# Turned attention weights: one transfer to DRAM and four back, in place of 16 transfers within SBUF

## The chip, the cores and the metric

The kernel runs on one core of one Trainium2 chip. The metric is the device time of one execution in microseconds (us); the figure is the median of three runs. The engines are called by the names that the profile uses: PE (TensorE, matrix products), DVE (VectorE), ACT (ScalarE), POOL (GpSimd) and SP (SyncE, which here does nothing but issue transfers). SPq is SP's queue of instructions, PEld the loading of weights into PE.

## The reference: what is computed

An attention that keeps only the 32 largest scores of each row, then a feed-forward block. All data are float32.

```python
B, H, S, D = 8, 8, 576, 64                    # batches, heads, sequence, head dim
scores = scale * q @ k.T                      # per batch and head: 576 x 576
kth    = np.partition(scores, -32)[..., -32]  # the 32nd largest of each row
scores = np.where(scores >= kth, scores, -1e9)
attn   = softmax(scores)                      # weights z: 576 queries x 576 keys
x      = (attn @ v)                           # then heads side by side: 4608 x 512
h      = x @ w_in                             # 4608 x 2048
out    = (h - np.tanh(h)) @ w_out             # 4608 x 512
```

## The kernel before

The kernel goes through the problem in 144 steps. A step takes 128 queries of two heads (of one batch), or the 64 queries that remain of two pairs of heads. A step runs through a pipeline over several iterations of one loop: scores on PE, the search for the 32nd largest score on DVE, mask and exponential on ACT and POOL, and then the product with v on PE. For that product the keys have to lie on the partitions, while the weights come out with the queries on the partitions. So the weights are turned.

For batch 0 PE turns them (`turn_pe`, steps with `pe`). For all others DVE turns each block of 32 x 32 within its group of 32 partitions, and transfers then bring the blocks to the groups where they belong. Two steps (a pair, `nq == 2`) share one such exchange; the remainders (`rem`, `nq == 1`) have one each.

```python
zx2 = [consts.tile([P, 4 * S], FP32, name="zx")[:], later[:, 0 : 4 * S]]   # two buffers
et_rem = later[:, 4 * S : 6 * S]          # "later" is part of the tile "spare"
etpool = pool("et", 1)                    # one buffer
G, NG = 32, 4                             # partitions in a group, groups
...
def turn_z(n):                            # DVE: turn 32 x 32 blocks
    g, z = steps[n], st.pop(n)["z"]
    ...
    nc.vector.transpose(
        tiles(zx, g.nq)[:, :, :, g.i, :].rearrange("p c k j -> p k c j"),
        z[:].rearrange("p (k c j) -> p k c j", c=NG, j=G),
    )

def spread_keys(n):                       # 16 transfers: group a, column block c
    zx = zxs.pop(n)                       #   -> group c, column block a
    rem = steps[n].rem
    et = ets[n] = et_rem if rem else etpool.tile([P, 4 * S], FP32, tag="et", name="et")
    w = steps[n].nq * S // 2              # 576 for a pair, 288 for a remainder
    for a in range(NG):
        for c in range(NG):
            nc.sync.dma_start(
                et[group(c), a * w : (a + 1) * w], zx[group(a), c * w : (c + 1) * w]
            )

def values(n):                            # PE: product with v, from et
    ...
    nc.tensor.matmul(av[half(t), 0, cols], vb[g.b, hp][:, t, c, :] ..., es[...], ...)
```

The order of instructions is fixed by hand. In iteration `n` of the loop stand, among others and in this order:

```python
    for m in (n - 4, n - 3):              # lag is 4 for steps turned by transfers
        if 0 <= m < NS and steps[m].last and steps[m].lag == n - m:
            values(m)                     # PE: weights of step n - 4
    ...
    if here(0):
        search(n, exact, between)         # DVE; after its first round: turn_z(n - 2)
    if here(-2) and not pe and steps[n - 2].last:
        spread_keys(n - 2)                # SP
    deal(...)                             # PE: a share of the feed-forward products
    if here(1):
        scores(n + 1)                     # PE
    ...
    for fn in todo.pop(n, []):
        fn()                              # SP: loads of k, q, v for later steps
```

So the weights of a pair are turned and sent out in iteration n and used at the start of iteration n + 2. `search` reads the scores straight from PSUM (one buffer there), so the scores of the next step wait for its first operations. All transfers of this stretch are issued by SP, in the order of the program: the exchange, the loads and the results.

Of the kernel before, what the change touches and what calls it, by code (L numbers as in the profile page):

```python
# [10 lines left out]
FP32 = mybir.dt.float32  # L11
# [37 lines left out]
def kernel(  # L49
# [9 lines left out]
    nc = tc.nc  # L59
    P = nc.NUM_PARTITIONS  # L60
# [10 lines left out]
    NG = P // G  # L71
    KC = 2 * S // P
    G = 32
    NG = P // G
# [8 lines left out]
    def pool(name, bufs, **kw):  # L83
        return ctx.enter_context(tc.tile_pool(name=name, bufs=bufs, **kw))
# [10 lines left out]
    xrpool = pool("xr", 1)  # L95
    thpool = pool("th", 4)
    gpool = pool("g", 4)
    sc_ps = pool("sc_ps", 1, space=PS)
    zt_ps = pool("zt_ps", 2, space=PS)
    h_ps = pool("h_ps", 2, space=PS)  # L100
# [260 lines left out]
    def group(a):  # L361
        return slice(a * G, (a + 1) * G)
# [18 lines left out]
    def spread_keys(n):  # L381


        zx = zxs.pop(n)
        rem = steps[n].rem
        et = ets[n] = et_rem if rem else etpool.tile([P, 4 * S], FP32, tag="et", name="et")
        w = steps[n].nq * S // 2
        for a in range(NG):
            for c in range(NG):
                nc.sync.dma_start(  # L390
                    et[group(c), a * w : (a + 1) * w], zx[group(a), c * w : (c + 1) * w]
                )

    def turn_pe(n):

# [137 lines left out]
    steps, done, work = [], {}, []  # L533
# [36 lines left out]
    def run(exact):  # L570
# [119 lines left out]
        for n in range(-4, NS + 4):  # L690
# [16 lines left out]
            if here(-2) and not pe and steps[n - 2].last:  # L707
                spread_keys(n - 2)
# [64 lines left out]
```

## Time and profile before

| What | before |
|---|---|
| time, median of 3 runs | 1543.8 us (1543.63 to 1544.71) |
| span of the profiled run | 1542.8 us |
| PE busy | 1440.7 us (93%) |
| DVE busy | 1347.2 us (87%) |
| ACT busy | 883.9 us (57%) |
| POOL busy | 940.8 us (61%) |
| bytes moved by DMA | 147.42 MB, mean 96 GB/s |
| exchange of a pair, `et<-zx` and `et<-spare` | 896 transfers of 72 KB |
| exchange of a remainder, `spare<-zx` and `spare<-spare` | 224 transfers of 36 KB |

How to read it: an engine's busy time is a sum over the whole span, and the span has stages. The weights of the feed-forward block are loaded and converted at the start, batch 0 is turned on PE, from about 255 us on the exchange is done by transfers, and in the last 100 us only PE has much left to do. A name such as `et<-zx` is a transfer or an operation that writes `et` and reads `zx`; `L390` is the line of the exchange in the kernel, `L376` the turn on DVE, `L433` the product with v, `L486` and `L507` the two products of the feed-forward block, `L237` the scores. The two buffers of `zx` appear under two names, `zx` and `spare`.

### The profile page before, as it was taken

To read this page: it belongs to the slowest core of one execution; us is meant where nothing else is said; L and a number is where in the kernel's file an instruction comes from. 1 tells how busy PE (TensorE), PEld (TensorE's weight loads), DVE (VectorE), ACT (ScalarE), POOL (GpSimd) and SP (SyncE) were. 2 spreads that over 40 slices of the span, in tenths; PEclk is the share of its full clock that TensorE was granted. 3 is DMA by queue.
4 is the path that set the end of the run, shared out by engine and by line. 5 is a ranking of instruction groups with operands and counts; after the bars stand their busy time and mean duration, and the time that the engine had idled before them with its cause. 6 is when DMAs were issued, how large, how long until landed. Compare 5 with 4: busy or idle time off the path is not lost.

```text
span 1542.8 us, 25300 instructions
## 1 busy us (share of the span) xinstructions
PE 1440.7 (93%) x7428; PEld 912.1 (59%) x7428; DVE 1347.2 (87%) x3828; ACT 883.9 (57%) x1567; POOL 940.8 (61%) x1525
## 2 busy tenths in 40 slices
PE   2567899999999999999999999999999999999997
PEld 1355566465666666656566665656566665656673
DVE  6998899999999999999999999999999999997300
ACT  4887776566555565556555565556555565655320
POOL 2777677567665665756565675757565675746420
PEclk9887999999999999999999999999999999999999
DMA  9944113324533354234433354234433344322200
GB/s 241 360 169 168 50 32 76 78 71 102 112 86 80 76 112 101 70 79 95 106 87 79 77 110 103 70 78 96 102 89 79 77 103 109 78 67 58 73 8 16
DMA packets 258835, 147.42 MB, mean 96 GB/s; under 512 B 210048, under 2 KB 217216, under 8 KB 258688
## 3 DMA queue, kind: packets, MB, share of 16 engines
q1 hardware_dynamic: 256912, 145.49, 38.5%
q8 instruction: 62, 1.02, 0.3%
q14 instruction: 85, 0.70, 0.1%
q10 hardware_dynamic: 1776, 0.22, 0.1%
HBM read 61.85 MB, written 9.44 MB: 46 GB/s over the span
## 4 chain that ended last, share of the span: by engine, by line
PE 73%; DVE 10%; SPq 5%; ACT 4%; DMA 2%; issue 2%; POOL 2%; DVEq 0%; ACTq 0%; POOLq 0%
PE ops L507 28%; PE hps L486 26%; PE av L433 9%; PE scps L237 8%; SPq L390 3%; DVE m L275 2%; DVE ab L278 2%; PE av L441 2%; SPq L200 2%; DMA zx<-in_moe_w_in_dram 1%; DVE spare L376 1%; PE zt L409 1%; DVE ab L267 1%; DVE ab L270 1%; DVE ab L268 1%
## 5 line engine op out<-in xcount | busy, mean ns | idle before, releaser
L507 PE MATMUL ops<-w_out,g 128*128 128x512 f32 x1152 | 520.5, 598 | 0.0
L486 PE MATMUL hps<-xT,w_in 128*128 128x256 f32 (+1 forms) x2176 | 471.4, 372 | 1.2 <-POOL xT L457 1.2
L275 DVE MAX8 m<-ab 128x8 f32<-128x288 f32 (+1 forms) x1152 | 465.8, 447 | 0.0
L310 POOL TENSOR_TENSOR z<-sc,z 128x576 f32<-128x576 f32 x288 | 400.2, 1411 | 77.4 <-ACT z L307 77.4
L486 PEld LDWEIGHTS hps<-xT,w_in 128*128 128x128 f32 x2176 | 390.7, 193 | 73.9 <-issue 23.4
L278 DVE MATCH_REPLACE8 ab<-m,ab 128x288 f32<-128x288 f32 x864 | 377.3, 446 | 0.0
L507 PEld LDWEIGHTS ops<-w_out,g 128*128 128x128 f32 x1152 | 211.4, 191 | 244.8 <-issue 240.7
L307 ACT ACTIVATE z<-sc,tb 128x576 f32<-128x576 f32 x288 | 207.6, 769 | 153.1 <-POOL tb L294 153.1
L500 POOL TENSOR_TENSOR g<-g,th 128x512 f32<-128x512 f32 x144 | 183.7, 1276 | 123.5 <-ACT g L499 113.2
L330 ACT ACTIVATE z<-z,nb 128x576 f32<-128x576 f32 x288 | 221.6, 773 | 8.8 <-POOL z L310 8.7
L245 ACT COPY sc<-scps 128x1152 f32<-128x1152 f32 x144 | 160.9, 1117 | 108.5 <-PE scps L237 106.5
L237 PE MATMUL scps<-kT,qT 64*128 64x288 f32 (+1 forms) x1280 | 188.1, 445 | 31.7 <-DVE qT L222 28.1
L237 PEld LDWEIGHTS scps<-kT,qT 64*128 64x128 f32 (+1 forms) x1280 | 101.6, 184 | 120.5 <-issue 60.5
L267 DVE TENSOR_TENSOR ab<-scps,sc 128x576 f32<-128x576 f32 x144 | 108.0, 750 | 69.3 <-POOL bad L314 54.1
L433 PE MATMUL av<-et,vb 128*64 128x256 f32 (+1 forms) x1088 | 131.8, 378 | 37.2 <-ACT et L412 30.4
L457 POOL TENSOR_TENSOR xT<-xs 128x256 f32<-128x256 f32 (+1 forms) x68 | 47.2, 695 | 166.8 <-ACT xs L445 166.8
L498 ACT ACTIVATE th<-hps 128x512 f32<-128x512 f32 x144 | 85.4, 593 | 106.6 <-PE hps L486 104.1
L445 ACT COPY xs<-av 128x512 f32<-128x512 f32 (+1 forms) x84 | 44.2, 526 | 170.2 <-PE av L441 170.2
L433 PEld LDWEIGHTS av<-et,vb 128*64 128x64 f32 x1088 | 75.2, 139 | 98.6 <-ACT et L412 32.5
L340 POOL TENSOR_SCALAR rd<-den 128x2 f32<-128x2 f32 x144 | 33.4, 232 | 140.5 <-ACT z L330 98.2
L270 DVE MAX8 ab<-ab 128x8 f32<-128x288 f32 x288 | 116.9, 448 | 0.0
L268 DVE TENSOR_TENSOR ab<-scps,sc 128x576 f32<-128x576 f32 x144 | 107.8, 749 | 0.0
(67 smaller groups left out, 1253.9 us busy)
## 6 DMA issues: line engine op xcount, KB each, us to landing
et<-spare SPq DMA_DIRECT2D x448, 72.0 KB, 2.0
et<-zx SPq DMA_DIRECT2D x448, 72.0 KB, 2.0
kin<-in_k_dram SPq DMA_DIRECT2D x116, 72.0 KB, 2.4
vb<-in_v_dram SPq DMA_DIRECT2D x64, 128.0 KB, 2.5
out_dram<-ot SPq DMA_DIRECT2D x32, 256.0 KB, 2.2
qin<-in_q_dram SPq DMA_DIRECT2D x113, 72.0 KB, 2.3
w_out<-in_moe_w_in_dram SPq DMA_DIRECT2D x10, 512.0 KB, 5.3
w_out<-in_moe_w_in_dram SPq DMA_DIRECT2D x10, 511.5 KB, 6.1
```

Source lines behind the costliest of these rows:

```text
L237: nc.tensor.matmul(ps[rows, t, s, 0:S2], qT[g.b, g.hp + i][half(t), qs], kT[g.b, g.hp + i][half(t), ks], start=True, stop=True,)
L245: nc.scalar.copy(sc[:], ps[:, :, :, 0:S2])
L270: nc.vector.max(ab[:, t, S2 : S2 + 8], lo[:, t, :])
L275: nc.vector.max(m[:, t, m8], last[t] if i == rounds - 1 else cur[t])
L278: nc.vector.match_replace(nxt[t], m[:, t, m8], cur[t], NEG)
L307: nc.scalar.activation(zv[:, t, :], scf[:, t, :], AF.Relu, bias=tb[:, t : t + 1], scale=-BIG)
L310: nc.gpsimd.tensor_tensor(zv[:, t, :], scf[:, t, :], zv[:, t, :], ALU.subtract)
L330: nc.scalar.activation(x["zv"][:, t, :], x["zv"][:, t, :], AF.Exp, bias=x["nb"][:, t : t + 1], scale=scale, accum_out=den[:, t : t + 1],)
L433: nc.tensor.matmul(av[half(t), 0, cols], vb[g.b, hp][:, t, c, :] if c < J else vr[g.b, hp][:, t, :], es[:, :, (J + 1) * t + c if c < J els ...
L486: nc.tensor.matmul(cur[u][:, s : s + w], w_in[j][:, c, fo : fo + P], u.xT[:, c, 0:w], start=(c == 0), stop=(c == CD - 1),)
L500: nc.gpsimd.tensor_tensor(g, g, th[:], ALU.subtract)
L507: nc.tensor.matmul(cur[u][:], u.g[o // 1024][:, o % 1024 // 512, o % 512 : o % 512 + P], w_out[f // FJ][:, f % FJ, :], start=(f == 0), sto ...
```

## The change

The exchange goes by way of DRAM. One transfer stores all 128 partitions of the turned blocks to a DRAM tile, as they lie. Then four transfers, one for each group of partitions, load from it: a partition of group c gets, from each of the four groups a, the row of 576 (or 288) values that stands in column block c. On the DRAM side a row can be taken from any place, so one transfer can gather what four did before. There are five transfers to issue in place of 16, and the load needs `et` free while the store does not. The load has to wait until the store has landed. Every byte is moved twice.

```diff
+    dpool = pool("d", 2, space=bass.MemoryType.DRAM)
...
         w = steps[n].nq * S // 2
-        for a in range(NG):
-            for c in range(NG):
-                nc.sync.dma_start(
-                    et[group(c), a * w : (a + 1) * w], zx[group(a), c * w : (c + 1) * w]
-                )
+        there = dpool.tile([P, NG * w], FP32, tag=f"there{steps[n].nq}", name="there")
+        nc.sync.dma_start(there[:], zx[:, 0 : NG * w])
+        for c in range(NG):
+            nc.sync.dma_start(
+                et[group(c), 0 : NG * w].rearrange("i (a x) -> i a x", a=NG),
+                there[:, c * w : (c + 1) * w].rearrange("(a i) x -> i a x", a=NG),
+            )
```

The DRAM tile has two buffers for each of its two sizes.

## The prediction

> **What bounds the kernel now.** I read the slices of the page first, to see whether one engine is full throughout, then split the span into stages, then listed the waits of TensorE (PE), and last laid single hand-overs out in time. The slices say that the kernel has an opening, a long even middle and a tail:
>
> ```profile
> PE   2567899999999999999999999999999999999997
> ...
> DVE  6998899999999999999999999999999999997300
> ```
>
> PE and VectorE (DVE) are both above 90% in most slices, so the digits can't say which one sets the pace. The turn by transfers starts near 255 us (batch 0 turns its weights on PE), so I split from 240 us on. The columns are: stretch, length, then busy us of PE, weight loads, DVE, ACT and POOL, granted clock, DMA share, GB/s.
>
> ```profile
> 240.00:440.00 200.00, 188.75 (x982) 120.99 (x982) 199.43 (x565) 117.22 (x210) 132.13 (x222) 1.00 0.39 88
> 440.00:1440.00 1000.00, 998.57 (x5065) 618.05 (x5064) 935.60 (x2660) 570.88 (x1005) 632.43 (x1046) 1.00 0.38 87
> ```
>
> From 240 to 440 us DVE has no gap (0.57 us idle of 200) and PE waits 11 us. From 440 to 1440 us PE has no gap (1.43 us idle of 1000) and DVE waits 64 us. Both stages are bound by an engine whose instructions the change leaves alone. The chain of waits must be read with this in mind:
>
> ```profile
> PE 73%; DVE 10%; SPq 5%; ACT 4%; DMA 2%; issue 2%; POOL 2%; DVEq 0%; ACTq 0%; POOLq 0%
> PE ops L507 28%; PE hps L486 26%; PE av L433 9%; PE scps L237 8%; SPq L390 3%; DVE m L275 2%; DVE ab L278 2%; PE av L441 2%; SPq L200 2%; DMA zx<-in_moe_w_in_dram 1%; DVE spare L376 1%; PE zt L409 1%; DVE ab L267 1%; DVE ab L270 1%; DVE ab L268 1%
> ```
>
> It gives 3% of the span, some 50 us, to issuing the 16 transfers (SPq L390). That looks like a prize. But most of those steps lie before 440 us, where DVE runs without a gap beside them. The waits of PE for the turned weights are all that can be won, and they are small:
>
> ```profile
> PE av L433 <- DMA et<-zx: 3.2, 2, 1.7
> ...
> PE av L433 <- DMA et<-spare: 2.9, 3, 1.4
> ```
>
> So many us in total, so many times, longest: 6.1 us in five waits, four of them before 440 us.
>
> Two hand-overs in time show the budget that the new route must keep. The first is in the DVE-bound stage, the second in the PE-bound one (start, us, engine, line):
>
> ```profile
> 310.38 10.01 SPq L390 DMA_DIRECT2D et<-zx  x16
> ...
> 317.69 1.39 DVE L376 STREAM_TRANSPOSE spare<-z 128x1152 f32<-128x1152 f32 x1
> ...
> 322.01 1.95 PE L433 MATMUL av<-et,vb 128*64 128x256 f32 x16 [1.50 <-DMA et<-zx]
> ```
>
> ```profile
> 804.74 1.35 DVE L376 STREAM_TRANSPOSE spare<-z 128x1152 f32<-128x1152 f32 x1
> ...
> 806.15 10.28 SPq L390 DMA_DIRECT2D et<-spare  x16
> ...
> 820.98 1.95 PE L433 MATMUL av<-et,vb 128*64 128x256 f32 x16
> ```
>
> In the first, the transpose that precedes the issue ends at 310.31; the last of the 16 lands at 321.19 (chain of waits, in order of time), 10.9 us later, and PE starts 0.8 us after that: 11.7 us, and PE stood for 1.5 of them. In the second the transpose ends at 806.09 and PE comes for the weights at 820.98, after 14.9 us, without a wait. Reading the other pairs after 440 us in the same way, from the end of the second transpose to PE's start, gives 14.7 to 16.3 us.
>
> [...] The trace has a duration for such things: a 72 KB transfer within SBUF takes 2.0 us to landing, a store of 256 KB to DRAM 2.2:
>
> ```profile
> et<-spare SPq DMA_DIRECT2D x448, 72.0 KB, 2.0
> ...
> kin<-in_k_dram SPq DMA_DIRECT2D x116, 72.0 KB, 2.4
> ...
> out_dram<-ot SPq DMA_DIRECT2D x32, 256.0 KB, 2.2
> ```
>
> [...] the packet records of the 2304 B rows between groups of 32 partitions have a median of 167 ns, 13.8 B/ns for each of 16 engines, while the 2048 B rows of a 128-partition store take 85 ns, 24 B/ns.
>
> **The change part by part.** A pair of query tiles moves 128 x 9216 B = 1.18 MB; there are 56 pairs (896 transfers of 72 KB / 16) and 14 remainders of half the size.
>
> Removed: 16 issues, one every 0.63 us, so 10.0 us of SyncE's queue for each pair; the last is issued 9.4 us after the first and lands 2.0 us later by the medians.
>
> Added, out: one store over all 128 partitions. Each engine moves 8 rows of 9216 B; at 24 B/ns that is 8 x 0.384 = 3.1 us. The fixed part, from the 256 KB store, is 2.2 less 8 rows x 0.085 = 1.5 us. Out lands 4.6 us after its issue.
>
> Added, back: four loads into 32 partitions each, 8 rows of 2304 B an engine. I take the slow 167 ns for them[...]: 8 x 0.167 = 1.34 us each, 5.35 us for four; the issues (0.6 us apart) keep ahead. The fixed part, from the 72 KB load of k, 2.4 us less its 36 packets of 13 ns = 1.9 us. The last lands 7.2 us after the first issue.
>
> Sum: 0.1 + 4.6 + 0.1 + 7.2 = 12.0 us from transpose to landing, against 10.9 before; 12.8 with PE's 0.8 us. A remainder: 3.0 + 4.6 = 7.6 us against 11.
>
> Against the budget: after 440 us there are at least 14.7 us, so all of it stays hidden and PE goes on without a gap: nothing won, nothing lost. Before 440 us PE, which already waits 1.0 to 1.7 us in some pairs, would wait about 1.1 us longer in some five of them; PE also waits 3.2 us there for DVE (its scores wait for the search), which this eats first, and the 1.7 us wait at 371 us goes with a remainder that lands earlier. I book +0.5 us.
>
> Moved: SyncE's queue. A pair now holds it for 4.7 + 4 x 0.63 = 7.2 us instead of 10.0, a remainder for 5.6 instead of 10. Where a remainder follows a pair one step later (a step is 9.6 us), the queue ran over: the pair at 420.57 was issued only at 422.92, and PE waited 1.04 us for it at 435, with no gap of PE afterwards to make it good; at 770 the queue ran 3.6 us late and cost 0.4 us. I book -1.4 us for these two.
>
> The DMA engines carry 3.1 + 5.35 = 8.4 us for a pair instead of 5.3, every 19.15 us: their share rises from 0.38 to some 0.55. That isn't full.
>
> The tail gets nothing: the last pair is issued at 1454.51 and lands by 1466, but PE comes for it at 1473.87, after its queue of output matmuls.
>
> Net: about -1 us of 1543.8, hence 1543.
>
> **The rivals.** First, the removed issue time is worth what the chain says, 50 us or 3%. For it speaks the chain alone; against it, DVE without a gap in the stage where those steps lie. It would make 1495. Second, the two trips become a wait on PE. The pairs leave 14.7 to 16.3 us, some 15.3 in the middle; if the way out and back with PE's 0.8 us takes longer, each us over costs some 48 us (the pairs after 440 us). A trip of 16 us would make 16.8 - 15.3 = 1.5 us a pair, 72 us in all, or about 1615. For it speaks that the new store is larger than any this trace shows and its 9216 B rows are new, and that k and q loads share the engines; against it, my sum leaves 1.9 us even at the tightest pair, and the loads of 512 KB over 128 partitions, issued two at a time, land in 3.7 to 6.1 us by most of their medians, in line with it. Third, the slack is used up only sometimes, behind bursts of loads: a few waits of 1 us, 1545 to 1555. Fourth, the loads back reach full rate (24 B/ns): about 10 us in all; PE's waits before 440 us vanish, but DVE holds that stage, so 1541.
>
> **Range and chances.** The first and fourth ways differ little in time, so the middle is narrow; the upper side is longer because a trip that overruns costs at every pair. 1543, with 1539 to 1551 for 8 in 10. Faster by 2% needs the first rival: 2%. Slower by 2% (over 1575) needs an overrun of 0.7 us at every pair: 7%. Within 2%: 91%.
>
> **What would show it.** Right: the out transfer lands 4 to 5.5 us after its issue, the last load back 11 to 13 us after the transpose; PE's idle time between 440 and 1440 us stays under 5 us; DVE's between 240 and 440 us under 2. SPq L390 shrinks or leaves the chain with no gain in time. Wrong: waits of PE av for DMA et of a microsecond at every pair (second rival), or a shorter stage before 440 us with DVE still full (then something slowed DVE that I don't see).

## The result and the profile after

| What | before | after |
|---|---|---|
| time, median of 6 runs each | 1544.5 us (1543.6 to 1545.3) | 1539.7 us (1537.9 to 1541.9) |
| ratio, with its 95% interval | | 0.9970 (0.9957 to 0.9983) |
| the same, in a second comparison (28 and 14 runs) | 1543.9 us | 1540.9 us, 0.998 (0.9972 to 0.9988) |
| span of the profiled run | 1542.8 us | 1540.1 us |
| bytes moved by DMA | 147.42 MB | 221.61 MB |

The change gains 3 to 5 us, 0.2 to 0.3%. The middle of the profile looks as it did. These are the slices of the page of after:

```profile
PE   2567898999999999999999999999999999999997
...
DVE  6988899999999999999999999999999999997300
```

and the two stages (stretch, length, busy us of PE, weight loads, DVE, ACT, POOL, clock, DMA share, GB/s):

```profile
240.00:440.00 200.00, 189.91 (x983) 120.88 (x982) 198.31 (x565) 117.26 (x210) 132.26 (x222) 0.99 0.57 147
440.00:1440.00 1000.00, 999.30 (x5067) 618.14 (x5066) 936.55 (x2662) 571.37 (x1007) 633.14 (x1048) 1.00 0.57 148
```

DVE still holds the first stage (1.7 us idle of 200) and PE the second (0.70 us idle of 1000, where it was 1.43). The DMA engines are busy 0.57 of the time instead of 0.38, and PE loses nothing by that in the second stage, as its 0.70 us of idle time show. The chain of waits:

```profile
PE 79%; DVE 7%; ACT 4%; DMA 3%; issue 2%; SPq 2%; POOL 2%; DVEq 0%; ACTq 0%; POOLq 0%
PE hps L489 30%; PE ops L510 29%; PE av L436 10%; PE scps L238 9%; DVE m L276 2%; DVE ab L279 2%; PE av L444 2%; SPq L201 1%; DMA et<-there 1%; ACT z L308 1%; ACT f L159 1%; PE zt L412 1%; DMA zx<-in_moe_w_in_dram 1%; DVE ab L268 1%; DVE ab L271 1%
```

The issue of the exchange (SPq L390, 3% or some 50 us before) has left the list. PE's share has grown from 73 to 79%, and the time has moved by 0.3%: the chain had named work that lay beside an engine without a gap. PE's waits for the turned weights are about as many us as before (6.1):

```profile
PE av L436 <- DMA et<-there: 6.7, 3, 3.5
```

These three waits all lie before 330 us. The two hand-overs that the prediction showed, in time, now of after:

```profile
310.86 1.34 DVE L377 STREAM_TRANSPOSE zx<-z 128x1152 f32<-128x1152 f32 x1
...
312.23 0.34 SPq L390 DMA_DIRECT2D there<-zx  x1
...
316.49 1.74 SPq L392 DMA_DIRECT2D et<-there  x4
...
324.29 1.95 PE L436 MATMUL av<-et,vb 128*64 128x256 f32 x16 [1.80 <-DMA et<-there]
```

```profile
804.42 1.35 DVE L377 STREAM_TRANSPOSE spare<-z 128x1152 f32<-128x1152 f32 x1
...
805.80 0.34 SPq L390 DMA_DIRECT2D there<-spare  x1
...
810.02 1.75 SPq L392 DMA_DIRECT2D et<-there  x4
...
820.65 1.95 PE L436 MATMUL av<-et,vb 128*64 128x256 f32 x16
```

In the first, PE starts 12.1 us after the end of the transpose (11.7 before). In the second it comes after 14.9 us, exactly as before, and finds the weights there. SyncE is free 6.0 us after it issued the store, where the 16 transfers took 10. The loads go out once the store has landed: in the first hand-over it lands 4.15 us after its issue (312.23 to 316.38 in the chain of waits), and they are issued at 316.49. The landings, from the list of issues:

```profile
et<-there SPq DMA_DIRECT2D x224, 288.0 KB, 5.3
there<-spare SPq DMA_DIRECT2D x28, 1152.0 KB, 4.2
```

### The profile page after: what moved, and what is told of

The parts are those of the page before. It is cut to its first block, busy times and chain, and to the rows that moved or that the text cites. A ratio compares the mean times of both kernels' runs of the same rounds, so it can differ in the third digit from the quotient of the medians.

```text
span 1540.1 us, 24174 instructions
## 1 busy us (share of the span) xinstructions
PE 1441.5 (94%) x7428; PEld 911.6 (59%) x7428; DVE 1346.9 (87%) x3828; ACT 883.4 (57%) x1567; POOL 940.9 (61%) x1525
## 2 busy tenths in 40 slices
DMA packets 255466, 221.61 MB, mean 144 GB/s; under 512 B 197728, under 2 KB 204896, under 8 KB 248160
## 3 DMA queue, kind: packets, MB, share of 16 engines
q1 hardware_dynamic: 253552, 219.75, 53.1%
## 4 chain that ended last, share of the span: by engine, by line
PE 79%; DVE 7%; ACT 4%; DMA 3%; issue 2%; SPq 2%; POOL 2%; DVEq 0%; ACTq 0%; POOLq 0%
PE hps L489 30%; PE ops L510 29%; PE av L436 10%; PE scps L238 9%; DVE m L276 2%; DVE ab L279 2%; PE av L444 2%; SPq L201 1%; DMA et<-there 1%; ACT z L308 1%; ACT f L159 1%; PE zt L412 1%; DMA zx<-in_moe_w_in_dram 1%; DVE ab L268 1%; DVE ab L271 1%
```

## How the spans were cut

Executions of one kernel differ by up to some 3 us in the opening, before the first exchange is issued. So I cut every profile at the same three instructions: the copy of scores on ACT that starts at 246.45 us in before, the one at 442.48 us, and the store of the last result. In us:

| profile | up to the first cut | exchange, DVE-bound | exchange, PE-bound and tail | after the last store |
|---|---|---|---|---|
| before | 246.45 | 196.03 | 1090.44 | 9.88 |
| before_again | 246.60 | 198.83 | 1091.49 | 9.78 |
| before_third | 243.53 | 197.16 | 1090.54 | 9.47 |
| skip_only (executes what before does) | 243.52 | 196.45 | 1091.10 | 8.73 |
| after | 246.55 | 195.90 | 1089.63 | 8.02 |
| again | 244.56 | 195.33 | 1089.86 | 7.55 |
| main_only (executes what after does) | 245.78 | 195.48 | 1089.67 | 7.27 |
| rem_only | 244.95 | 194.49 | 1089.45 | 9.21 |
| pairs_only | 244.65 | 196.48 | 1089.44 | 10.43 |
| two_stores | 244.82 | 193.59 | 1089.44 | 7.55 |
| two_again | 245.20 | 192.85 | 1089.45 | 7.50 |
| four_stores | 244.31 | 192.84 | 1089.45 | 7.70 |
| queue_held | 245.13 | 202.03 | 1100.84 | 7.30 |

The first four lines against the next three, by their means: -1.5 us in the second column, -1.2 in the third, -1.9 in the last. The first column, which no transfer of the change can touch, differs by 0.6 us the other way. So of 4.6 us, 2.7 are won in the steps and 1.9 at the end of the program. The means are of four and of three profiles, and those of before spread over 2.8 us in the second column; but each of the three lies below each of the four there.

The second column has three parts, parted at the copies of scores that start at 328.19 and 383.17 us in before (us; the first two lines are the means of the same four and three profiles):

| profiles | up to 328 us | up to 383 us | up to 442 us |
|---|---|---|---|
| exchange by the 16 transfers | 82.1 | 55.6 | 59.4 |
| exchange by DRAM | 83.5 | 53.0 | 59.1 |
| rem_only | 82.6 | 53.0 | 58.9 |
| pairs_only | 83.4 | 53.1 | 60.0 |
| two_stores, two_again | 81.5, 80.8 | 53.3, 53.1 | 58.8, 58.9 |

Up to 328 us the change loses 1.4 us, and in the next part it gains 2.6. There the four profiles of the first line have a wait of PE of 1.75 to 2.1 us (near 371 us) for the exchange of a remainder, which no other profile of this table has.

## The experiments

My theory after the result was that the gain in the steps comes from SyncE's queue, which no longer runs late (queue theory). The rivals were that each exchange gains or loses by the length of its own trip (trip theory), and that the difference isn't in the steps but in the end of the program.

**The changed kernel again, and before again.** Nothing is edited.

> The changed kernel once more, nothing edited. Its first profile is 2.7 us shorter than that of before, 0.8 us of it before the last result is stored and 1.9 us after. If the gain lies in the steps (queue theory), the second profile shows the steps shorter by 1 to 4 us and the time stays at 0.996 to 0.998 of before. If it lies in the program's end, which is free to differ between executions, the end after the last store differs between the two profiles of the changed kernel by a microsecond or more, and the ratio moves towards 0.999.

> The kernel before, nothing edited, for a second profile of it. If the end of the program after the last result is stored (9.9 us in the first profile of before, 8.0 and 7.5 us in two profiles of the changed kernel) belongs to the program, it is 9.9 us again within 0.5. If it belongs to the single execution, it differs by a microsecond or more. The opening up to 240 us differs between executions by up to 2 us and does so here too.

> The kernel before once more, for a third profile of it. In its first two the steps from 246 us to the last store differ by 3.9 us, and the end after the last store is 9.9 and 9.8 us; in three profiles with the exchange by way of DRAM the steps lie within 0.4 us of each other and the end is 7.3 to 8.0 us. If the end belongs to the kernel, it is 9 to 10 us again. If the steps of before are the ones that vary, they come out anywhere between the first two.

The second profile of after has the same steps within 0.4 us in sum (1285.5 and 1285.2 us for the second and third columns), and its end is 7.55 us. Before gives 1286.5, 1290.3 and 1287.7 us, with ends of 9.88, 9.78 and 9.47: it varies more in the steps, and its end is its own within 0.5 us. So the end belongs to the kernel and not to the execution, and the first profile of before was the quickest of three in the steps: comparing the two first profiles alone (0.9 us in the steps) had understated the gain.

**Which exchanges matter.** In one kernel only the remainders go by DRAM, in the other only the pairs:

```diff
+        if not rem:        # rem_only; "if rem:" in pairs_only
+            for a in range(NG):
+                for c in range(NG):
+                    nc.sync.dma_start(
+                        et[group(c), a * w : (a + 1) * w], zx[group(a), c * w : (c + 1) * w]
+                    )
+            return
         there = dpool.tile([P, NG * w], FP32, tag=f"there{steps[n].nq}", name="there")
```

> Only the 14 remainders go by way of DRAM, the 56 pairs keep their 16 transfers. Queue theory: the remainders are what makes the queue run late (a remainder follows a pair one step later), so most of the gain comes back: the waits of PE at 371, 435, 782 and 1130 us go, 1541 to 1542.5 us. Trip theory (each exchange gains or loses by its own length): PE still waits 1 to 1.7 us for pairs between 260 and 330 us as before, and the gain is at most 1 us.

> Only the 56 pairs go by way of DRAM, the 14 remainders keep their 16 transfers. Queue theory: a pair frees the queue 3 us earlier, so half of the lateness goes: 1541.5 to 1543.5 us. Trip theory: all of the loss before 330 us is here (PE waits of 1.4 to 3.5 us) and none of the gain at 371 us: 1543 to 1546 us.

rem_only: 1537.8 us, 0.9957 (0.9943 to 0.9971). pairs_only: 1543.5 us, 0.9996 (0.9988 to 1.0004), no difference. A fifth of the exchanges, of half the size, brings at least as much as the whole change; the pairs alone bring nothing that the time shows. (That rem_only is faster than the whole change rests on the medians, 1537.8 against 1540.9 us; its profiled execution was the slowest of its five, and there steps and end take 1293.2 us, as much as in after.) The queue of SyncE shows why. This is before, around a pair and the remainder that follows one step later:

```profile
739.23 10.04 SPq L390 DMA_DIRECT2D et<-spare  x16
749.37 2.21 SPq L200 DMA_DIRECT2D qin<-in_q_dram  x4
751.68 11.35 SPq L390 DMA_DIRECT2D spare<-zx  x16
...
770.47 10.56 SPq L390 DMA_DIRECT2D et<-spare  x16
```

and this is after:

```profile
740.22 0.35 SPq L390 DMA_DIRECT2D there<-spare  x1
744.86 1.74 SPq L392 DMA_DIRECT2D et<-there  x4
746.69 2.74 SPq L201 DMA_DIRECT2D qin<-in_q_dram  x4
749.52 2.80 SPq L390 DMA_DIRECT2D there<-zx  x1
755.07 1.74 SPq L392 DMA_DIRECT2D spare<-there  x4
...
767.02 0.35 SPq L390 DMA_DIRECT2D there<-spare  x1
```

Two exchanges of 10 to 11 us and the loads between and behind them fill the queue, and the next pair goes out at 770.47, 3.6 us after its transpose; PE waits 0.4 us for it. After, the remainder is done with the queue at 756.8 in place of 763.0, and the next pair goes out at once. Freeing the queue at the remainders is enough for this, and it leaves the pairs their shorter trip (11.7 us from transpose to PE in the first hand-over, where it is 12.1 after). The expectation for rem_only (1541 to 1542.5 us) was too small by 3 us and more; that for pairs_only doesn't tell the theories apart, as its time fits both ranges. Its profile has something of both: PE waits 7.9 us for pairs in five places up to 434 us, as the trip theory says, but the wait at 371 us is gone, which that theory left in place, since the remainders keep their own way. In rem_only, which also loses that wait, the remainder's own way is shorter too; the waits behind it, near 435, 782 and 1130 us, are for pairs that kept the 16 transfers, and their going speaks for the queue alone.

**The queue alone.** The data take the new way, and the queue is held as long as before:

```diff
+        for i in range(8 if rem else 6):
+            nc.sync.dma_start(held[0:G, i : i + 1], ones[0:G, :])
```

> The changed kernel, and after the four loads of a pair 6 more transfers of 4 bytes a partition (8 for a remainder) that nobody uses, so that SyncE's queue is held for about as long as by the 16 transfers of before. The data take the same way. Queue theory: the gain goes, 1542.5 to 1545 us, and PE's wait at 435 us comes back. If the gain has nothing to do with the queue: 1539 to 1541 us, like the changed kernel.

1555.8 us, 1.0075 (1.0052 to 1.0098), outside both ranges: the gain is gone, and 12 us more. PE waits for the exchange in eight more places, at 386, 406, 438, 615, 790, 968, 1144 and 1319 us, 13.9 us in all, and DVE waits for k, whose loads stand in the same queue, four times in this part (3.6 us). The queue around the pair that after shows at 744.86:

```profile
746.14 0.44 SPq L391 DMA_DIRECT2D there<-spare  x1
750.88 1.73 SPq L393 DMA_DIRECT2D et<-there  x4
752.66 3.73 SPq L398 DMA_DIRECT2D held<-ones  x6
757.32 2.68 SPq L202 DMA_DIRECT2D qin<-in_q_dram  x4
```

Here a pair has the queue for 11.2 us (746.14 to 757.32), a microsecond more than the 10.0 of before, so this kernel isn't a clean return to before. It shows the direction and that the queue is near its limit: the data's way is that of after, and holding the queue costs 15 us against it.

**The length of the trip.** The store is cut so that the first loads wait for a part of it only:

```diff
-        nc.sync.dma_start(there[:], zx[:, 0 : NG * w])
+        for s in range(2):
+            nc.sync.dma_start(there[s], zx[:, 2 * s * w : (2 * s + 2) * w])
```

with a DRAM tile of shape [2, P, NG * w // 2] and loads from `there[c // 2]`; four_stores goes on to one store for each column block.

> The changed kernel with the store cut into two, each of two column blocks, so that the first two loads wait only for the first half. The way out and back should be 1 to 1.5 us shorter (the first half lands after about 3 us in place of 4.2), for one issue more. If PE's waits before 330 us come from the length of the trip, they shrink by about 1 us each and the time by 0.5 to 1.5 us against the changed kernel. If not, it stays within 0.5 us of it or gets longer by the issue.

> Two stores once more, on another chip or at another time, to narrow its interval. If the shorter trip is what brought it from 0.998 to 0.995, it is 0.994 to 0.9965 again. If that was the luck of five runs, it moves to 0.998.

> The store cut into four, one for each column block, each load waiting only for its own. Trip theory: the first load can start still earlier (about 2.5 us after the first store instead of 2.9 with two), but eight issues hold SyncE's queue longer; the loads are the longer part, so little is left to win: 1536.5 to 1538.5 us, like two stores. If the trip's length is all that counts, a further 0.5 us less; if the queue counts more, 1538.5 to 1541 us.

two_stores: 1537.3 us, 0.9952 (0.9938 to 0.9966), and the second time 1536.8 us, 0.9957 (0.9944 to 0.9971). four_stores: 1537.8 us, 0.9967 (0.9954 to 0.9979). Against 0.998 (0.9972 to 0.9988) for the changed kernel, two stores are faster by 0.28 and 0.23% (by 0.18 and 0.13% against the 0.997 of its first comparison), some 2 to 4 us where 0.5 to 1.5 were expected; four add nothing. In two_stores the hand-over of above reads

```profile
308.02 1.35 DVE L377 STREAM_TRANSPOSE zx<-z 128x1152 f32<-128x1152 f32 x1
...
309.39 0.81 SPq L391 DMA_DIRECT2D there<-zx  x2
...
312.27 2.17 SPq L393 DMA_DIRECT2D et<-there  x4
...
316.76 1.37 DVE L377 STREAM_TRANSPOSE spare<-z 128x1152 f32<-128x1152 f32 x1
...
320.15 1.95 PE L437 MATMUL av<-et,vb 128*64 128x256 f32 x16 [0.58 <-DMA et<-there]
```

The loads go out 2.9 us after the store in place of 4.3, and PE starts 10.8 us after the transpose in place of 12.1. The table has the gain where it was expected: the DVE-bound stretch is 2.0 to 2.7 us shorter than in after, the PE-bound one 0.3. So both theories hold, in different places. Up to 328 us the trip counts, since PE is waiting for it: the change loses 1.4 us there, and the divided store wins that and more back. At 371 us and later the lateness of the queue counts, as long as the trip fits into the slack.

**A trip that is too long.** One more copy within DRAM, between the store and the loads:

```diff
+        hop = dpool.tile([P, NG * w], FP32, tag=f"hop{steps[n].nq}", name="hop")
+        nc.sync.dma_start(hop[:], there[:])
+        there = hop
```

> The changed kernel with one more copy, from the DRAM tile to a second DRAM tile, between the store and the loads. The copy of 1.18 MB should take 4 to 5 us, so that from the end of the transpose to PE it would be 12.1 + 4.5 = 16.6 us, against the 14.7 to 16.3 us that PE leaves after 440 us. Second rival of the prediction (a trip longer than the slack costs at every pair): PE waits about 1 us at nearly each of the 47 pairs after 440 us, more where the queue runs late, 1585 to 1640 us. If the slack grows with the delay (DVE and the loads shift too), far less: under 1560 us.

1679.5 us, 1.0906 (1.0874 to 1.0939), 40 us beyond the expected range, which had left out the stage before 440 us: there the profile is 37 us longer than those of the changed kernel. The copy takes 5.5 us to landing, and SyncE waits for it too:

```profile
833.24 1.35 DVE L377 STREAM_TRANSPOSE spare<-z 128x1152 f32<-128x1152 f32 x1
...
835.62 0.44 SPq L390 DMA_DIRECT2D there<-spare  x1
...
840.04 0.50 SPq L392 DMA_DIRECT2D hop<-there  x1
...
845.46 1.74 SPq L395 DMA_DIRECT2D et<-hop  x4
...
853.35 2.49 PE L439 MATMUL av<-et,vb 128*64 128x256 f32 x16 [3.37 <-DMA et<-hop]
```

PE starts 18.8 us after the transpose here: 1.0 us before the store is issued, because the queue runs late again, 9.8 us of two trips, then the loads. The wait is 3.4 us, and the 16 products take 2.49 us where they take 1.95 elsewhere. The stage:

```profile
440.00:1500.00 1060.00, 982.93 (x4902) 616.76 (x4902) 902.59 (x2559) 553.64 (x974) 613.65 (x1017) 0.97 0.67 190
```

PE idles 77 us of 1060, and its clock is granted at 0.97. The copy also holds SyncE's queue, for 11.6 us a pair (835.62 to 847.20). In queue_held 11.2 us a pair cost 15 us, so most of the 139 us against the changed kernel belongs to the trip, though this run does not part the two. The second rival of the prediction was real; the changed kernel stays clear of it by the slack of the pairs.

**The end of the program.** The kernel ends in a branch that skips a second pass (for inputs on which the search has to be done exactly). In one kernel only that skipped pass has the new exchange, in the other only the executed pass:

```diff
+        if not second[0]:      # skip_only; "if second[0]:" in main_only
+            ...                # the 16 transfers, then return
```

`second[0]` is set while the second pass is being written out.

> The exchange of the executed pass is that of before; only in the second pass, which stands behind a branch and is never executed on these inputs, does it go by way of DRAM. What runs is the kernel before; the code that is skipped at the end is 770 transfers shorter. Theory that the end of the program carries some 2 us of the gain by the amount of skipped code: the end after the last store takes 7.5 to 8.5 us, 1541 to 1542.5 us. Theory that all of the gain is in the steps: like before, 1543.5 to 1545 us.

> The counterpart: the executed pass goes by way of DRAM, the skipped pass keeps the 16 transfers. Theory of the end: the end takes 9 to 10 us as before and only the steps gain, 1542 to 1543.5 us. Theory of the steps: like the changed kernel, 1539.5 to 1541 us.

skip_only: 1542.4 us, 0.9991 (0.9978 to 1.0004), no difference shown; the time itself lies in the range of the first theory, the ratio fits both. main_only: 1540.6 us, 0.9978 (0.9968 to 0.9988), like the changed kernel. The ends are 8.73 and 7.27 us. The theory that the amount of skipped code sets the end is down: with the short skipped pass the end is longer than with the long one. Over all profiles of the table the end is 7.3 to 8.0 us where every executed exchange goes by DRAM, and 8.7 to 10.4 us where some are the 16 transfers. The instructions in the traces show where it lies. The closing sequence of semaphores and drains begins 4.2 to 4.5 us after the issue of the last store where some exchanges are the 16 transfers, and after 3.6 to 3.8 us where none is; within it no engine starts anything for 2.0 to 3.2 us in the former, for 0.8 to 1.5 us in the latter. What makes that difference I don't know; it stays open.

## Why the prediction was right, and where its sizes were off

The forecast was 1543 us, 1 us less than before; the time is 1539.7.

- "Both stages are bound by an engine whose instructions the change leaves alone": right after 440 us, where PE idles 0.70 us of 1000; the 50 us that the chain put on the issue of transfers came to under 3 us. Before 440 us it holds in part. DVE stays full (1.7 us idle of 200), and yet the stage got 1.5 us shorter, which the prediction had named as a sign of being wrong. Nothing slowed DVE in before: its mean instruction takes 0.35 us in both. The stretch up to the copy at 442 us is PE's busy and idle time, and the idle time went from 10.7 to 11.7 us in the four profiles of the 16 transfers to 9.2 to 10.1 in the three by DRAM. DVE has done 556 or 557 instructions in the stretch then in place of 561 to 563, and makes up for it in the next stage, where it idled 64 us. So DVE without a gap did not hide the waits of PE, which is full in the next stage.
- The trip: 12.0 us to landing was predicted, and in the hand-over above 12.0 came out (312.20 to 324.16), partly by luck. The way out is shorter than assumed, 4.2 us by the median in place of 4.6: its 9216 B rows take 352 ns, 26.2 B/ns, where I had taken 24. The way back is longer, 7.7 us from the first issue to the last landing in place of 7.2, and its packets of 2304 B take 184 ns by the median in place of 167, 12.5 B/ns; that they would run at the rate of the 16 transfers was my estimate, and what sets it is not shown. The trip of before was misread: what lands at 321.19 is the fifteenth transfer. The last, issued at 319.81, lands at 321.82, after 11.5 us and not 10.9, and PE starts 0.2 us later, not 0.8. So PE starts 12.1 us after the transpose in place of 11.7, later by 0.4 us and not by 1.1.
- "The slack of 14.7 to 16.3 us hides it": right. No wait of PE for a pair after 440 us shows in the profile of after, one of 0.36 us in again and one of 0.17 us in main_only, and extra_hop shows what happens beyond the slack. With this the third rival, a few waits of 1 us, is out too.
- "+0.5 us before 440 us", net of what is saved at 371 us, and "-1.0 us" for the late queue at 420 us: together -0.5, measured -1.5 by the means. The sizes failed. The longer trip costs 1.4 us up to 328 us, the wait that goes at 371 us brings 2.6 us (2.2 without before_again, whose PE clock was granted at 0.50 from 372.55 to 375.96 us, right after it) where 1.7 was counted, and the last part, with the late queue, brings 0.3 where 1.0 was booked.
- "-1.4 us for the queue", of which -0.4 after 440 us: that part measures -1.2 us by the means. The waits are those I had named, behind a remainder; before_again has 1.03 us at 786 us and 0.76 at 1134. They make up about half: 0.8 us by the mean of the four profiles, 0.2 in the three.
- The end of the program, -1.9 us, was not in the sum at all. I had no term for it, and no run explains it. Without it the gain is 2.7 us, where the sum had 1.
- DMA share 0.55 predicted, 0.57 measured, and harmless, as said.
- The tail got nothing, as said: PE goes from its output products to the last pair without a wait in both kernels.

The fourth rival (loads at 24 B/ns) is out, although its 1541 us is the nearest to the time: the loads run at 12.5 B/ns for each engine. The first (the chain's 3%) is out.

## What to carry to other kernels

A chain of waits that runs through a queue is worth only what the engine beside it leaves open: look for gaps in the engine that is full in that stage, and towards its end in the one that is full in the next, before counting on it (here the chain gave the issue some 50 us, and the steps won 2.7). A queue of transfers pays by being on time for what stands behind it: replacing the few exchanges that come right after another one was worth at least as much as replacing all of them (1537.8 us against 1540.9). Where a transfer has to wait for another, cutting the first so that the second can start on a part of it shortened the trip by 1.3 us (10.8 in place of 12.1) at the cost of one more issue (0.81 us for both in place of 0.34).

## What I had not expected of the hardware

A short wait of PE cost more than the wait. At the first exchange PE waits 1.4 to 3.5 us, depending on the execution, and in some of them the 16 products after it take over 3 us. Two profiles with nearly the same wait, skip_only first, then before_third:

```profile
266.16 1.95 PE L443 MATMUL av<-et,vb 128*64 128x256 f32 x16 [2.08 <-DMA et<-spare]
```

```profile
266.25 3.63 PE L433 MATMUL av<-et,vb 128*64 128x256 f32 x16 [2.16 <-DMA et<-spare]
```

and the stretch around it in each, where the third figure from the end is the granted clock:

```profile
262.00:276.00 14.00, 11.92 (x66) 8.94 (x65) 14.00 (x43) 8.07 (x18) 8.30 (x12) 1.00 0.32 74
```

```profile
262.00:276.00 14.00, 11.84 (x60) 8.58 (x59) 14.00 (x42) 6.31 (x13) 6.54 (x9) 0.88 0.32 74
```

In thirteen profiles of this place the clock stays at 1.00 with waits of 1.4 to 2.08 us and is 0.88 with waits of 2.16 to 3.5 us (in extra_hop the wait is 8.7 us and the clock 0.70). But the length of the wait does not decide. Near 370 us a wait of 1.99 us is followed by a lower clock in before_again, one of 2.11 us is not in before_third; the columns are those of the stages above:

```profile
369.13:372.55 3.42, 1.43 (x34) 1.08 (x35) 3.42 (x12) 0.00 (x0) 0.67 (x1) 1.00 0.37 76
372.55:375.96 3.41, 3.41 (x19) 1.76 (x15) 3.41 (x11) 1.25 (x3) 1.38 (x6) 0.50 0.86 138
```

```profile
365.32:368.74 3.42, 1.62 (x23) 0.72 (x21) 3.42 (x11) 0.00 (x0) 1.24 (x1) 1.00 0.21 51
368.74:372.15 3.41, 3.09 (x33) 1.73 (x37) 3.41 (x11) 0.95 (x2) 1.36 (x5) 1.00 0.83 135
```

From 200 us on the clock is granted at one half in stretches of 3.41 us (in extra_hop also of two or three such lengths), and within one profile they begin whole multiples of 3.41 us apart (270.15 and 372.55 us in before_again). If all fourteen profiles are divided by that grid, PE was busy for at most 0.42 of the interval before each of the 34 falls to one half, and no interval at full clock in which it was busy for 0.45 or more is followed by a fall. In the first pair of lines that share is 1.43 of 3.42, in the second 1.62, since the wait lies across the end of the interval. So PE need not have been idle for the whole interval before a fall; what makes the clock fall is not shown beyond this.

Each fall costs the stage before 440 us about 1.7 us of PE: up to the copy at 442 us PE is busy for 184.8 us in before and skip_only, which have none, 186.5 in before_third with one and 188.0 in before_again with two.

The issue of a transfer on SyncE did not take longer for more bytes, by the medians: 0.34 us for a store of 1.18 MB to DRAM, 0.42 for a load of 288 KB, and 0.59 for 72 KB within SBUF. Single issues took longer (2.80 us for the store of 576 KB at 749.52 us in after). What sets it is not shown.
